# Prologue of a spectral layer with an MLP behind it: first-stage results kept in the memory of later weights, loop data loaded in four pieces, half of batch 2's first stage put into the main loop

## The chip, the core and the metric

One core of one Trainium2 chip runs the whole program. The metric is the device time of one execution in microseconds (us), the median of several runs. The engines are named as in the profile: PE (matmul) and PEld (its weight loads), DVE, ACT, POOL, and SP, which here only issues DMA transfers.

## What is computed

The input x is 4 batches of 3008 positions with 256 channels. Cut to what matters, the reference is:

```python
X = np.fft.rfft(x, axis=1)
Yr = Xr @ w_r - Xi @ w_i + b_r
Yi = Xr @ w_i + Xi @ w_r + b_i
Yr, Yi = softshrink(Yr, 0.01), softshrink(Yi, 0.01)
y = np.fft.irfft(Yr + 1j * Yi, n=3008, axis=1).reshape(12032, 256)
h = y @ w_in                       # 256 -> 2048
P = a[0] + a[1]*h + a[2]*h**2 + a[3]*h**3
Q = 1 + |b[0]|*|h| + |b[1]|*h**2
out = (P / (Q + 1e-6)) @ w_out     # 2048 -> 256
```

The MLP's weights w_in, w_out come as 64-bit floats and are turned on the chip into pairs of 32-bit values (a rounded high part and the rest).

## The kernel before

**The transform.** 3008 = 64 x 47. A batch passes five steps. The first stage (`f1_task`) is a transform over 47 points, 16 tasks of one matmul each, two tasks for each of 8 pieces of x; its result `a` is stored to a DRAM scratch `s1`, since the next step wants other rows on the partitions. `f2_task` (12 tasks) loads `s1` back as `bt`, does the 64-point transform with the table `f2`, and ACT makes a high part, PE (L222) and ACT a low part, and ACT (L218) a negated copy. `m_task` is the complex product with the weights, 24 matmuls and one for the bias, and the soft threshold (ACT L246, DVE L249). `i1_task` transforms back with the table `g1`, and its result `zt` is copied out of PSUM by ACT (L149) and stored to a second scratch `s2`. `i2_task` loads `s2` as `ct` and makes columns of y for the MLP.

**Prologue and main loop.** Batch 1 (`b == 0` in the code) passes f1 to i1 in a prologue, in which the MLP's weights are also loaded and converted (`more_raw` issues loads, `convert(n)` takes n steps of a conversion; 16 conversions of 5 steps; one costs ACT three instructions and DVE four). Its order is written out by hand: for each p from 0 to 14 the code runs f2 of p, m of p-2, i1 of p-3, with `HC[p]` and `HM[p]` conversion steps between. Batch 2 (`b == 1`) has all 16 first-stage tasks in the prologue: two before the loop over p, six in its first three passes, eight behind it. The main loop then runs 208 units (26 blocks of columns x 8 slices of the hidden layer): 12 matmuls L321 into `h`, a rational function on ACT, POOL and DVE, 12 matmuls L412 into `acc`, three units later. The tasks of batches 2 to 4 are dealt out to these units by a budget: each task has a cost in us, and a unit takes tasks until it has its share of the sum, at most two at a time.

**Memory and queues.** Every DMA is issued by SP, in program order, on one queue. The framework gives the queue's transfers eight semaphores in turn, so an issue waits until the eighth transfer before it has landed. Tiles with one tag share a ring of buffers: `zt` has the tag "a" with three buffers in the pool `sm`, so the fourth result waits until the first has been stored. `a` of the prologue has five buffers of its own in the pool `pro` plus two lent places. The weights' tiles (tags "win0" to "win7", "wsp0" to "wsp7") lie in memory for good and are empty until the weights come; pieces 2 to 7 of x use the "win" places already. Before the loop over p, 20 matmuls on zeros (`warm`, L483) keep PE busy.

Of the kernel before, what the change touches and what calls it, by code (L numbers as in the profile page):

```python
# [30 lines left out]
RAWS = (2, 2, 2, 2, 2, 2, 2, 0, 0, 0, 0, 0)  # L31
HC = (0, 3, 3, 4, 4, 4, 4, 4, 4, 4, 4, 4)
HM = (0, 0, 3, 3, 3, 3, 4, 4, 4, 4, 4, 4, 4, 4)
# [62 lines left out]
def spectral_moe(ctx, tc, t, out):  # L96
# [53 lines left out]

    def f1_task(b, i):
# [28 lines left out]
    def load_b(b, p):  # L180
        if b or p < 2:
            bt = sm.tile([128, 2, D], F32, tag="b", name="bt")
        else:
            bt = pro3.tile([128, 2, D], F32, tag="b", name="bt", bufs=4)
# [11 lines left out]
    def f2_task(b, p):  # L196
        ahead = 2 if b else 3
        if p + ahead < NK // 2:
            late.append(lambda: load_b(b, p + ahead))
        bt = b_t.pop((b, p))  # L200
# [17 lines left out]
        nc.scalar.activation(out=every[:, :, :64], in_=v32(every[:, :, 128:]), func=ACTF.Copy, scale=-1.0)  # L218
# [33 lines left out]
    def i1_task(b, p):  # L252
# [8 lines left out]
        copy(0, zt.rearrange("p k d -> p (k d)"), pt.rearrange("p k d -> p (k d)"))  # L261
# [180 lines left out]
    raw_pool = pro_stack.enter_context(tc.tile_pool(name="raw", bufs=max(len(WHOLE), 1)))  # L442
# [30 lines left out]
    with tc.manual_schedule():  # L473
        nc.vector.memset(cb, 1.0)
        nc.scalar.activation(out=cb, in_=cb, func=ACTF.Abs_reciprocal_sqrt)
        nc.sync.dma_start(out=f1, in_=t["f1"])
        idle = pro.tile([128, 512], mybir.dt.bfloat16, tag="idle", name="idle", bufs=1)
# [70 lines left out]
        for i in range(8, 16):  # L548
            drain(f1_task(0, i))
# [8 lines left out]
        nc.sync.dma_start(out=eye, in_=t["minus"])  # L558
        first = fft_tasks(1)
        begin_f1 = [first.pop(0)[3] for _ in range(2)]  # L560
        for g in begin_f1:
            next(g)
            next(g)
        prepare()
        load_b(0, 0)
        load_x(1, 1)
        load_b(0, 1)
        nc.sync.dma_start(out=f2[:, 4:8], in_=f2_src[:, 4:8])
        load_b(0, 2)
        load_x(1, 2)  # L570
        load_x(1, 3)
        for g in begin_f1:
            drain(g)
        more_raw(2)
        warm(20)
        np_ = NK // 2
        for p in range(np_ + 3):
            if p < np_:
# [3 lines left out]
                sl = slice(2 * p + 8, 2 * p + 10)  # L582
                if p < np_ - 4:
                    nc.sync.dma_start(out=f2[:, sl], in_=f2_src[:, sl])
                sl = slice(2 * p, 2 * p + 2)
                nc.sync.dma_start(out=g1[:, sl], in_=g1_src[:, sl])
            if p < 3:
                for _ in range(2):
                    drain(first.pop(0)[3])
# [12 lines left out]
            if p == 3:  # L602
# [147 lines left out]
```

## Time and profile before

| | before |
|---|---|
| median of 3 runs | 1498.27 us (1498.03 to 1498.34) |
| profiled execution | 1502.75 us, its span 1500.9 us |
| PE busy | 1469.2 us, 98% of the span |
| DVE busy | 1377.1 us, 92% |
| ACT busy | 1298.0 us, 86% |
| chain that ended last | PE 83%, DVE 7%, ACT 4%, issue 3%, DMA 2% |

The chain is the work followed back from the last instruction to what released each step. A busy share is a mean over stages with different limits, so a stage's own limit is read from a table of the busy times in that stage.

### The profile page before, as it was taken

The numbers are of one execution on the slowest core, as the hardware profiler recorded it, in microseconds if no ns is written. First come the engines' busy times: TensorE is split into PE (matmuls) and PEld (weight loads), VectorE is DVE, ScalarE is ACT, GpSimd is POOL, SyncE is SP. The second block draws the span as 40 slices with busy tenths as digits, with TensorE's granted clock in tenths as the row PEclk, the third lists the DMA queues.
The fourth block names the chain that finished last, engine by engine and source line by source line (L and its number), as shares of the span: only waits on it lengthen the run. The fifth ranks groups of instructions, "written<-read, shape, count | busy, mean of one in ns | idle before, by whom it ended". The sixth has DMA issues, their size and how long they took to land.

```text
span 1500.9 us, 19717 instructions
## 1 busy us (share of the span) xinstructions
PE 1469.2 (98%) x7335; PEld 1225.8 (82%) x7335; DVE 1377.1 (92%) x1328; ACT 1298.0 (86%) x1550; POOL 470.0 (31%) x218
## 2 busy tenths in 40 slices
PE   8989999999999999999999999999998999999998
PEld 3786999998878999999888998999886777776776
DVE  1563999999999999999999999999999999999998
ACT  4777989888989888898899988998887999999886
POOL 0001233323333233233233323332345333333332
PEclk9999999999999999999999999999999999999999
DMA  8954010111232011011132101011010000000000
GB/s 253 359 157 131 23 55 28 55 43 40 62 114 74 28 42 55 28 56 41 57 111 76 35 28 55 28 35 41 28 40 13 27 14 27 27 13 27 9 13 21
DMA packets 56431, 88.72 MB, mean 59 GB/s; under 512 B 5544, under 2 KB 40176, under 8 KB 56336
## 3 DMA queue, kind: packets, MB, share of 16 engines
q1 hardware_dynamic: 56336, 87.46, 18.8%
q8 instruction: 58, 0.95, 0.3%
q14 instruction: 37, 0.30, 0.1%
HBM read 49.96 MB, written 37.49 MB: 58 GB/s over the span
## 4 chain that ended last, share of the span: by engine, by line
PE 83%; DVE 7%; ACT 4%; issue 3%; DMA 2%; SPq 0%; ACTq 0%; DVEq 0%
PE acc L412 32%; PE h L321 31%; PE pft L240 7%; PE pi L291 3%; PE pft L156 3%; PE pft L204 2%; PE pft L258 2%; DMA s<-a 1%; DVE t L359 1%; DMA xin<-in_x 1%; DVE v L382 1%; DVE t L376 1%; DVE y L384 1%; DVE p L374 1%; PE pm L240 1%
## 5 line engine op out<-in xcount | busy, mean ns | idle before, releaser
L348 POOL TENSOR_TENSOR v<-w,m 128x940 f32<-128x940 f32 (+1 forms) x208 | 456.9, 2196 | 1019.2 <-DVE p L374 485.2
L321 PE MATMUL h<-xsh,win 128*128 128x470 f32 (+1 forms) x1664 | 448.8, 391 | 2.6 <-DVE t L361 2.4
L412 PE MATMUL acc<-g,wsp 128*128 128x470 f32 (+1 forms) x1908 | 433.7, 375 | 5.1 <-DVE g L379 5.1
L412 PEld LDWEIGHTS acc<-g,wsp 128*128 128x128 f32 x1908 | 358.3, 189 | 54.8 <-DVE g L379 7.1
L321 PEld LDWEIGHTS h<-xsh,win 128*128 128x128 f32 x1664 | 303.9, 189 | 61.0 <-issue 20.6
L361 DVE SCALAR_TENSOR_TENSOR t<-t,small,h 128x940 f32<-128x940 f32 (+1 forms) x208 | 244.9, 1177 | 6.1
L346 ACT ACTIVATE w<-m,small 128x940 f32<-128x940 f32 (+1 forms) x208 | 241.6, 1162 | 7.0
L359 DVE TENSOR_TENSOR t<-t,h 128x940 f32<-128x940 f32 (+1 forms) x208 | 231.2, 1111 | 16.4 <-ACT t L347 16.1
L321 PE MATMUL h<-xsl,win 128*128 128x470 f32 (+1 forms) x832 | 242.1, 372 | 0.0
L353 ACT ACTIVATE y<-v 128x940 f32<-128x940 f32 (+1 forms) x208 | 202.8, 975 | 37.0 <-DVE g L379 28.3
L347 ACT ACTIVATE t<-h,small 128x940 f32<-128x940 f32 (+1 forms) x208 | 229.8, 1105 | 0.0
L354 ACT ACTIVATE y<-y 128x940 f32<-128x940 f32 (+1 forms) x208 | 203.8, 980 | 6.6
L344 ACT ACTIVATE m<-h 128x940 f32<-128x940 f32 (+1 forms) x208 | 194.5, 935 | 16.4 <-PE h L321 13.6
L379 DVE TENSOR_TENSOR g<-t,y 128x940 fp32r<-128x940 f32 x159 | 179.5, 1129 | 18.0 <-PE acc L412 16.3
L371 DVE SCALAR_TENSOR_TENSOR g<-t,small,y 128x940 fp32r<-128x940 f32 x159 | 191.9, 1207 | 1.1 <-ACT y L354 1.1
L376 DVE SCALAR_TENSOR_TENSOR t<-t,small,p 128x940 f32<-128x940 f32 x159 | 189.5, 1192 | 0.0
L374 DVE SCALAR_TENSOR_TENSOR p<-v,g 128x940 f32<-128x940 f32 x159 | 179.0, 1126 | 0.1
L321 PEld LDWEIGHTS h<-xsl,win 128*128 128x128 f32 x832 | 155.3, 188 | 20.9 <-DVE xsl L302 0.2
L412 PE MATMUL acc<-g,f 128*128 128x470 f32 (+1 forms) x392 | 155.7, 539 | 2.5 <-DVE g L388 2.5
L412 PEld LDWEIGHTS acc<-g,f 128*128 128x128 f32 x392 | 73.3, 189 | 60.8 <-issue 54.6
L240 PE MATMUL pft<-wrh,x 128*128 128x256 f32 x288 | 75.3, 283 | 0.0
L240 PE MATMUL pft<-wih,x 128*128 128x256 f32 x288 | 75.2, 283 | 0.0
(84 smaller groups left out, 1437.2 us busy)
## 6 DMA issues: line engine op xcount, KB each, us to landing
xin<-in_x SPq DMA_DIRECT2D x32, 384.0 KB, 4.7
s<-a SPq DMA_DIRECT2D x64, 192.0 KB, 3.4
bt<-s SPq DMA_DIRECT2D x48, 256.0 KB, 3.0
s<-zt SPq DMA_DIRECT2D x48, 256.0 KB, 2.2
out_t<-ob SPq DMA_DIRECT2D x50, 235.0 KB, 2.3
ct<-s SPq DMA_DIRECT2D x22, 480.0 KB, 4.2
raw_win<-in_w_in SPq DMA_DIRECT2D x8, 512.0 KB, 6.9
raw_wsp<-in_w_out SPq DMA_DIRECT2D x8, 512.0 KB, 7.1
```

What stands on the lines that cost most here:

```text
L240: nc.tensor.matmul(out=pt[:, k, :], lhsT=l, rhs=r, start=False, stop=n == len(ops) - 1, skip_group_check=True)
L321: nc.tensor.matmul(out=h[:, i, :w], lhsT=l, rhs=r, start=k == 0, stop=k == len(ops) - 1)
L344: nc.scalar.activation(out=d["m"], in_=h, func=ACTF.Abs)
L346: nc.scalar.activation(out=d["w"], in_=d["m"], func=ACTF.Identity, scale=cb[:, 1:2], bias=cb[:, 0:1])
L347: nc.scalar.activation(out=d["t"], in_=h, func=ACTF.Identity, scale=a[:, 3:4], bias=a[:, 2:3])
L348: nc.gpsimd.tensor_tensor(out=d["v"], in0=d["w"], in1=d["m"], op=ALU.mult)
L353: nc.scalar.activation(out=d["y"], in_=d["v"], func=ACTF.Square, bias=C0)
L354: nc.scalar.activation(out=d["y"], in_=d["y"], func=ACTF.Abs_reciprocal_sqrt)
L359: nc.vector.tensor_tensor(out=tt, in0=tt, in1=h, op=ALU.mult)
L361: nc.vector.scalar_tensor_tensor(out=tt, in0=tt, scalar=d["a"][:, 1:2], in1=h, op0=ALU.add, op1=ALU.mult)
L376: stt(out=tt, in0=tt, scalar=a0, in1=p, op0=ALU.add, op1=ALU.subtract)
L412: nc.tensor.matmul(out=acc[n][e][:, :w], lhsT=l[:, e * 128:(e + 1) * 128], rhs=r, start=begun[n] == 1 and k == 0, stop=begun[n] == UB and ...
```

## The change

Eight pieces of `a` of batch 1 (two tasks each, 4 KB a partition) go to the places "wsp0" to "wsp7" and are stored whole, by turns copied by ACT and DVE. No load of batch 2's x stands among them. `bt` of batch 1 is loaded as four tiles `b_all` of six rows each, f2 and g1 in two or three pieces each, and all 16 raw weights, and then pieces 0 to 3 of batch 2's x, are issued ahead of the loop over p. In batch 1 the negated copy goes from ACT to POOL, the copy of `zt` from ACT to DVE. `warm` grows from 20 to 36. Of batch 2's first stage, eight tasks run behind the loop over p, with `a` in the three buffers of "a" in `sm`, and eight are left to the main loop.

```diff
-RAWS = (2, 2, 2, 2, 2, 2, 2, 0, 0, 0, 0, 0)
-HC = (0, 3, 3, 4, 4, 4, 4, 4, 4, 4, 4, 4)
-HM = (0, 0, 3, 3, 3, 3, 4, 4, 4, 4, 4, 4, 4, 4)
+HC = (0, 0, 3, 3, 3, 3, 3, 3, 3, 3, 3, 3)
+HM = (0, 0, 4, 4, 4, 4, 4, 4, 4, 4, 4, 4, 4, 4)
...
-        if b == 0 and i % 7 >= 5:
-            at = const.tile([128, 4, D], F32, tag="win1" if i % 7 == 5 else f"wsp{SPLIT[0]}", name="a")[:96, :2]
+        if b == 0:
+            if not r:
+                a_t[0] = const.tile([128, 4, D], F32, tag=f"wsp{c}", name="a")[:96]
+            at = a_t[0][:, 2 * r:2 * r + 2]
         else:
-            at = (pro if early else sm).tile([128, 2, D], F32, tag="a", name="a", bufs=5 if early else 3)[:96]
-        copy(0, at.rearrange("p j d -> p (j d)"), pt[:96])
+            at = sm.tile([128, 2, D], F32, tag="a", name="a", bufs=3)[:96]
+        copy(i % 2 if b == 0 else 0, at.rearrange("p j d -> p (j d)"), pt[:96])
         yield
         if r:
             del xin[b, c]
-            if c < 6 and b > 1:
-                load_x(b, c + 2)
+            ahead = 4 if b == 1 and c < 4 else 2
+            if b and c + ahead < NJ // 4 and not (b == 1 and c in (2, 3)):
+                load_x(b, c + ahead)
...
-        nc.scalar.activation(out=every[:, :, :64], in_=v32(every[:, :, 128:]), func=ACTF.Copy, scale=-1.0)
+        if b:
+            nc.scalar.activation(out=every[:, :, :64], in_=v32(every[:, :, 128:]), func=ACTF.Copy, scale=-1.0)
+        else:
+            nc.gpsimd.tensor_scalar(out=every[:, :, :64], in0=v32(every[:, :, 128:]), scalar1=-1.0, scalar2=0.0, op0=ALU.mult, op1=ALU.add)
...
-        copy(0, zt.rearrange("p k d -> p (k d)"), pt.rearrange("p k d -> p (k d)"))
+        copy(b == 0, zt.rearrange("p k d -> p (k d)"), pt.rearrange("p k d -> p (k d)"))
...
+        b_all = [pro3.tile([128, 6, D], F32, tag=f"b{z}", name="b_all", bufs=1) for z in range(4)]
...
+        for i in range(16):
+            drain(f1_task(0, i))
+        prepare()
...
+        nc.sync.dma_start(out=f2[:, 4:12], in_=f2_src[:, 4:12])
+        load_all(0)
+        load_all(6)
+        more_raw(2)
+        load_g1(slice(0, 8))
+        nc.sync.dma_start(out=f2[:, 12:], in_=f2_src[:, 12:])
+        load_all(12)
+        more_raw(2)
+        load_g1(slice(8, NK))
+        load_all(18)
...
+        more_raw(len(jobs))
+        for c in range(4):
+            load_x(1, c)
+        warm(36)
...
-        while first[0][0]:
+        for _ in range(8):
             drain(first.pop(0)[3])
-        del first[:2]
-        load_b(1, 0)
-        load_b(1, 1)
```

**The queue of SP around the first results.** In the kernel before, inside the loop over p, a store of `zt` (to `s_472`, which is `s2` of batch 1) stands between the loads of one pass:

```order
L264 DMA s_472<-zt 128x2x256
L185 DMA bt<-s_125 128x2x256
L517 DMA raw_wsp_493<-in_w_out 128x2x256
L517 DMA raw_wsp_495<-in_w_out 128x2x256
L584 DMA f_70<-in_f 128x256
L586 DMA g_71<-in_g 128x256
```

In the changed kernel, at the end of the loads that stand ahead of the loop (`s_428` is `s2` of batch 1, `s_1005` is `s1` of batch 2):

```order
L525 DMA raw_wsp_253<-in_w_out 128x2x256
L525 DMA raw_wsp_255<-in_w_out 128x2x256
L141 DMA xin<-in_x 96x1024 x4
L271 DMA s_428<-zt 128x2x256 x12
L283 DMA ct<-s_428 96x1280
L178 DMA s_1005<-a 96x512
L141 DMA xin<-in_x 96x1024
L178 DMA s_1005<-a 96x512 x2
```

All twelve stores of `zt` now stand behind all loads of weights and four pieces of x, and the stores of batch 2's `a` behind `ct`, with loads of x between them.

**The engine that copies the fourth `zt`.** Before, on ACT, in pass 6 (its waits in brackets: HW3 is the semaphore of the first store):

```order
L246 ACTIVATE yt<-pm 128x512 [waits PE_49]
L469 ACTIVATE win_669<-e 128x2x256 [waits DVE_49]
L214 ACTIVATE x<-pft 128x4x128 [waits PE_49]
L218 ACTIVATE x<-x 128x8x64 [waits Activation_49]
L149 ACTIVATE zt<-pft 128x512 [waits DMAHW3_49,PE_49]
L208 ACTIVATE x<-pft 128x4x128 [waits PE_49]
```

Now, on DVE, in the same pass (HW7 is the semaphore of the first store):

```order
L256 SCALAR_TENSOR_TENSOR yt<-pm,yt 128x512 [waits Activation_49]
L478 TENSOR_TENSOR win_563<-e,win_563 128x2x256 [waits DVE_49]
L465 SCALAR_TENSOR_TENSOR e<-raw_win_237,e 128x512 [waits DMAHW1_49,DVE_49]
L471 ISA e<-e,r 128x1024 [waits DVE_49]
L146 COPY zt<-pft 128x512 [waits DMAHW7_49,PE_49]
L463 TENSOR_SCALAR e<-e 128x512 [waits Activation_49]
L478 TENSOR_TENSOR win_602<-e,win_602 128x2x256 [waits Activation_49]
L465 SCALAR_TENSOR_TENSOR e<-raw_win_239,e 128x512 [waits DMAHW2_49,DVE_49]
L256 SCALAR_TENSOR_TENSOR yt<-pm,yt 128x512 [waits Activation_49]
```

The copy and its wait for the first store have moved to DVE, ahead of the conversions and of the next soft threshold.

**PE where the main loop begins.** Before, from the last eight first-stage tasks (each row x8 is eight matmuls of 512 columns):

```order
L156 MATMUL pft<-xin,small 96x512 x8
L291 MATMUL pi_1146<-small,ct 128x94 x5
L291 MATMUL pi_1152<-small,ct 128x94 x5
L321 MATMUL h<-xsh,win_370 128x470 x4
L321 MATMUL h<-xsl,win_370 128x470 x2
L321 MATMUL h<-xsh,win_370 128x470 x4
L321 MATMUL h<-xsl,win_370 128x470 x2
L204 MATMUL pft<-f_70,bt 128x128 x8
L321 MATMUL h<-xsh,win_427 128x470 x4
```

Now, from the same place:

```order
L157 MATMUL pft<-xin,small 96x512 x8
L298 MATMUL pi_1061<-small,ct 128x94 x5
L298 MATMUL pi_1067<-small,ct 128x94 x5
L328 MATMUL h<-xsh,win_367 128x470 x4
L328 MATMUL h<-xsl,win_367 128x470 x2
L328 MATMUL h<-xsh,win_367 128x470 x4
L328 MATMUL h<-xsl,win_367 128x470 x2
L157 MATMUL pft<-xin,small 96x512 x2
L328 MATMUL h<-xsh,win_387 128x470 x4
```

Eight first-stage tasks stand in both ahead of the loop; the changed kernel has two more in each of units 0 to 3, where the kernel before has second-stage and product tasks of batch 2, which now begin in unit 5.

## Rows read from the trace of the kernel before

**Rows 1.** Busy time of each engine in stretches (start:end, length, then PE, PEld, DVE, ACT and POOL busy us with their instruction counts, granted clock, DMA share, GB/s): the start of the loop over p, its steady part, its end to the first matmul of the main loop, the main loop's first units, the main loop up to the end of batch 4's transform.

```profile
32.70:46.60 13.90, 11.21 (x39) 6.35 (x37) 4.08 (x8) 5.59 (x10) 0.00 (x0) 0.75 1.03 348
46.60:103.70 57.10, 51.16 (x370) 47.74 (x369) 37.34 (x66) 49.34 (x94) 0.00 (x0) 1.00 0.84 273
103.70:125.30 21.60, 20.26 (x100) 14.68 (x99) 5.81 (x10) 11.25 (x21) 0.00 (x0) 0.92 0.42 131
125.30:161.70 36.40, 34.29 (x209) 30.65 (x208) 22.72 (x24) 31.06 (x41) 8.88 (x4) 1.00 0.24 76
161.70:1093.00 931.30, 931.30 (x4909) 825.05 (x4909) 908.25 (x845) 831.77 (x970) 302.54 (x136) 1.00 0.16 50
```

**Rows 2.** Timeline of PE from the last product of batch 1 to the first units: start us, duration us, engine, line, instruction, count, and idle time of the engine before it with what ended it.

```profile
109.19 0.58 PE L233 MATMUL pm<-bias,selr 128*128 128x512 f32 x1
...
115.02 7.03 PE L156 MATMUL pft<-xin,small 96*96 96x512 f32 x16
122.47 1.32 PE L291 MATMUL pi<-small,ct 96*128 96x94 f32 x10 [0.41 <-DMA ct<-s]
...
125.31 0.67 PE L321 MATMUL h<-xsh,win 128*128 128x470 f32 x2
...
130.08 1.13 PE L204 MATMUL pft<-f,bt 128*128 128x128 f32 x8 [1.46 <-DMA bt<-s]
```

**Rows 3.** Timeline of PE over one pass of the loop over p without a wait (columns as in Rows 2).

```profile
61.57 0.47 PE L233 MATMUL pm<-bias,selr 128*128 128x512 f32 x1
...
65.85 1.05 PE L204 MATMUL pft<-f,bt 128*128 128x128 f32 x8
66.66 0.47 PE L233 MATMUL pm<-bias,selr 128*128 128x512 f32 x1
```

**Rows 4.** Timeline of SP, PE and ACT in the first 30 us (columns as in Rows 2).

```profile
1.19 3.87 SPq L142 DMA_DIRECT2D xin<-in_x  x8
...
5.67 9.65 PE L156 MATMUL pft<-xin,small 96*96 96x512 f32 x22 [1.28 <-DMA xin<-in_x]
...
18.65 2.05 ACT L149 ACTIVATE a<-pft 96x512 f32<-96x512 f32 x4 [6.13 <-DMA s<-a]
...
19.30 9.30 PE L156 MATMUL pft<-xin,small 96*96 96x512 f32 x14 [3.97 <-ACT a L149]
```

**Rows 5.** The same table as in Rows 1 for three short stretches: the loads of x, the loads of weights, `bt`, f2 and g1 in the loop, and PE after a wait.

```profile
4.00:16.00 12.00, 10.04 (x23) 3.50 (x22) 0.00 (x0) 4.14 (x7) 0.00 (x0) 1.00 1.04 258
45.00:60.00 15.00, 14.99 (x103) 13.09 (x102) 9.77 (x17) 12.56 (x24) 0.00 (x0) 0.97 1.06 384
40.00:45.00 5.00, 5.00 (x13) 2.89 (x12) 0.71 (x2) 2.30 (x4) 0.00 (x0) 0.50 1.06 390
```

**Rows 6.** DMA issues of three moments, each a window that holds one issue (KB, us from issue to landing): a store of `zt` at 65.64 us with the queue full, one at 102.18 us with the queue empty, a load of `bt` at 29.80 us.

```profile
s<-zt SPq DMA_DIRECT2D x1, 256.0 KB, 6.2
...
s<-zt SPq DMA_DIRECT2D x1, 256.0 KB, 2.1
...
bt<-s SPq DMA_DIRECT2D x1, 256.0 KB, 2.8
```

**Rows 7.** Groups of POOL instructions of the whole program: line, instruction, count, busy us, mean ns of one, idle us before them.

```profile
L717 POOL TENSOR_TENSOR f<-wsp 128x512 f32<-128x512 f32 x6 | 13.2, 2208 | 0.0
```

**Rows 8.** Timeline of ACT at the end of the prologue (columns as in Rows 2).

```profile
115.27 0.60 ACT L149 ACTIVATE zt<-pft 128x512 f32<-128x512 f32 x1 [1.13 <-PE pft L258]
...
123.04 1.56 ACT L149 ACTIVATE a<-pft 96x512 f32<-96x512 f32 x3 [2.93 <-DMA s<-a]
124.49 0.57 ACT L294 ACTIVATE xsh<-pi 128x470 fp32r<-128x470 f32 x1
```

**Rows 9.** Groups of DVE instructions between 46 and 116 us (columns as in Rows 7).

```profile
L464 DVE CUSTOM_DVE_ANT_0 e<-e,r 128x1024 uint16<-128x1024 uint16 x16 | 11.0, 688 | 0.3
L249 DVE SCALAR_TENSOR_TENSOR yt<-pm,yt 128x512 f32<-128x512 f32 x12 | 8.3, 689 | 15.2 <-ACT yt L246 15.2
L456 DVE TENSOR_SCALAR e<-e 128x512 uint32<-128x512 uint32 x15 | 6.3, 421 | 3.5 <-ACT e L453 3.5
L471 DVE TENSOR_TENSOR win<-e,win 128x512 fp32r<-128x512 f32 x8 | 5.5, 690 | 2.7 <-ACT win L469 2.7
...
L458 DVE SCALAR_TENSOR_TENSOR e<-raw_wsp,e 128x512 uint32<-128x512 uint32 x8 | 5.5, 684 | 0.0
```

**Rows 10.** Timeline of SP's queue at the same place.

```profile
118.10 0.33 SPq L276 DMA_DIRECT2D ct<-s  x1
118.47 6.46 SPq L170 DMA_DIRECT2D s<-a  x8
```

**Rows 11.** Timeline of PE from the twelve matmuls of unit 1 to what follows them.

```profile
131.86 1.11 PE L321 MATMUL h<-xsh,win 128*128 128x470 f32 x4
...
134.53 0.63 PE L222 MATMUL pft<-x,minus 128*128 128x512 f32 x2
135.61 0.50 PE L233 MATMUL pft<-bias,selr 128*128 128x512 f32 x1 [0.45 <-ACT x L214]
```

**Rows 12.** Timeline of DVE: the first instruction of a unit's DVE work in units 0, 4 and 5.

```profile
131.92 1.13 DVE L359 TENSOR_TENSOR t<-t,h 128x940 f32<-128x940 f32 x1 [5.12 <-ACT t L347]
...
161.69 1.13 DVE L359 TENSOR_TENSOR t<-t,h 128x940 f32<-128x940 f32 x1
...
168.28 1.13 DVE L359 TENSOR_TENSOR t<-t,h 128x940 f32<-128x940 f32 x1
```

More of the change, by code (lines that the diff above doesn't have):

```diff
@@ L135, in load_x @@
     def load_x(b, c):
-        if b == 1 and c in (2, 3, 6, 7):
-            xt = pro3.tile([96, 4, D], F32, tag=f"x{c % 4}", name="xin", bufs=1)
+        if b == 1 and c in (2, 3):
+            xt = pro3.tile([96, 4, D], F32, tag=f"x{c}", name="xin", bufs=1)
         elif b == 0 and c >= 2:
@@ L149, in copy @@
             nc.scalar.activation(out=out, in_=in_, func=ACTF.Copy)
+    a_t = {}
     def f1_task(b, i):
@@ L166, in f1_task @@
             del xin[b, c]
-            if c < 6 and b > 1:
-                load_x(b, c + 2)
+            ahead = 4 if b == 1 and c < 4 else 2
+            if b and c + ahead < NJ // 4 and not (b == 1 and c in (2, 3)):
+                load_x(b, c + ahead)
+        if b == 0:
+            if r:
+                nc.sync.dma_start(out=s1[b].rearrange("k g c j d -> (k g c) j d")[:, 4 * c:4 * c + 4, :], in_=a_t[0])
+            return
         o = 4 * c + 2 * r
@@ L180, in load_b @@
     def load_b(b, p):
[L181 to L184, printed above, removed]
+        bt = sm.tile([128, 2, D], F32, tag="b", name="bt")
         nc.sync.dma_start(out=bt, in_=s1[b][2 * p:2 * p + 2].rearrange("k g c j d -> (g c j) k d"))
@@ L196, in f2_task @@
     def f2_task(b, p):
[L197 to L200, printed above, removed]
+        if b and p + 2 < NK // 2:
+            late.append(lambda: load_b(b, p + 2))
+        bt = b_t.pop((b, p)) if b else b_all[p // 3][:, 2 * (p % 3):2 * (p % 3) + 2]
         pt = bank(b, "f2" if p % 2 else "").rearrange("p (z f) -> p z f", z=4)
@@ L441, in spectral_moe @@
     pro3 = pro_stack.enter_context(tc.tile_pool(name="pro3", bufs=3))
-    raw_pool = pro_stack.enter_context(tc.tile_pool(name="raw", bufs=max(len(WHOLE), 1)))
+    raw_pool = pro_stack.enter_context(tc.tile_pool(name="raw", bufs=len(WHOLE))) if WHOLE else None
     pro2 = pro_stack.enter_context(tc.tile_pool(name="pro2", bufs=2))
@@ L539, in spectral_moe @@
         nc.sync.dma_start(out=f2[:, :4], in_=f2_src[:, :4])
-        load_x(1, 0)
-        for i in range(8):
-            drain(f1_task(0, i))
         wts = []
@@ L547, in spectral_moe @@
             wts.append(wt)
-        for i in range(8, 16):
-            drain(f1_task(0, i))
         sel = pro.tile([4, 130], F32, tag="sel", name="sel", bufs=1)
@@ L558, in spectral_moe, with load_all, load_g1 @@
         nc.sync.dma_start(out=eye, in_=t["minus"])
-        first = fft_tasks(1)
[L560 to L576, printed above, removed]
+        for i in range(16):
+            drain(f1_task(0, i))
+        prepare()
+        np_ = NK // 2
+        def load_all(k):
+            nc.sync.dma_start(out=b_all[k // 6], in_=s1[0][k:k + 6].rearrange("k g c j d -> (g c j) k d"))
+        def load_g1(sl):
+            nc.sync.dma_start(out=g1[:, sl], in_=g1_src[:, sl])
+        nc.sync.dma_start(out=f2[:, 4:12], in_=f2_src[:, 4:12])
[8 more added lines that the diff above has]
+        load_all(18)
+        nc.sync.dma_start(out=ca, in_=t["a"].rearrange("(o d) -> o d", o=1).to_broadcast([128, 4]))
+        nc.sync.dma_start(out=cb, in_=t["b"].rearrange("(o d) -> o d", o=1).to_broadcast([128, 2]))
+        nc.sync.dma_start(out=i2, in_=t["i2"])
+        more_raw(len(jobs))
+        for c in range(4):
+            load_x(1, c)
+        warm(36)
+        first = fft_tasks(1)
         for p in range(np_ + 3):
@@ L581, in spectral_moe @@
                 next(f2g)
[L582 to L589, printed above, removed]
             flush()
             if p < np_:
-                more_raw(RAWS[p])
                 convert(HC[p])
@@ L601, in spectral_moe @@
                 drain(i1_task(0, p - 3))
-            if p == 3:
-                nc.sync.dma_start(out=ca, in_=t["a"].rearrange("(o d) -> o d", o=1).to_broadcast([128, 4]))
-                nc.sync.dma_start(out=cb, in_=t["b"].rearrange("(o d) -> o d", o=1).to_broadcast([128, 2]))
-                nc.sync.dma_start(out=i2, in_=t["i2"])
-            if 6 <= p < 10:
-                load_x(1, p - 2)
             if p == 8:
@@ L611, in spectral_moe @@
         flush()
-        more_raw(len(jobs))
         while running or len(done) < len(jobs):
```

## The prediction

> **What bounds the kernel now.** First read the table of busy times by stage [rows 1]. From 161.7 to 1093 us PE is busy for all of its time (931.30 of 931.30 us), with DVE close behind (908.25). There, work added to PE counts in full. Ahead of it stand a prologue of 125.3 us, in which no engine is full, and the first units, where PE idles 36.40 - 34.29 = 2.1 us. The prologue is where a new order can gain. Its PE work at full clock is small: two times sixteen first-stage tasks at 7.03 / 8 = 0.88 us [rows 2], twelve passes at 66.66 - 61.57 = 5.1 us [rows 3] and 2.2 us of i2, about 91 us. So some 34 us are lost: a start of 5.7 us, a wait of 4.0 us for a store that holds a buffer [rows 4], waits and half clock from 32.7 to 46.6 us (clock 0.75 [rows 1]), and shorter waits behind.
>
> **First stage and its stores.** The waits of ACT (6.13 us) and PE (3.97 us) for `s<-a` [rows 4] go, as eight places hold all of `a`. What is late next is the queue. The eight pieces of x (3.15 MB) arrive at 258 GB/s [rows 5], from about 4 to 16.2 us, as before. Then follow 0.26 MB of f2, 0.52 MB of weights and 3.15 MB of stores: at the 384 GB/s of the busy stretch [rows 5] 10.2 us, landed at about 27. The first quarter of `b_all` (0.79 MB) needs all stores. A load of 0.26 MB took 2.8 us [rows 6], so 2.1 us besides its bytes; with 2.0 us of bytes it lands at 31. The loop begins where it begins now, near 32; what is gained is that nothing of batch 2 stands in it.
>
> **The queue behind it.** In the order now, the first store of `zt` stands behind every weight and four pieces of x. After 31 us there are 13.1 MB (three quarters of `b_all`, 16 raw weights, g1, the rest of f2): 34.1 us at 384 GB/s, so 65. Four pieces of x at 258 GB/s add 6.1 us, the store's own bytes 0.7 and its landing 1.0: it lands at **73 us**. That the queue works in order rests on two stores of the same size, 6.2 us from issue to landing with others ahead, 2.1 us with none [rows 6]. Bounds: 70 us if x moves at 384 GB/s too and the gap ahead of the first quarter is filled; 81 us if all pieces with rows of 4 KB or more (stores, f2, g1, 6.0 MB) move at the 258 GB/s of x.
>
> The Trainium skill, "DMA: Bandwidth & Descriptors", section Bandwidth, says "Batch DMAs to ≥1 MiB for ≥75% of peak" and lists 425 GB/s for 16 MB. The trace differs: pieces of 128 to 512 KB already ran at 384 GB/s. By that best rate, as an estimate, the store would land near 66 us and the whole would come to 1499 us; rival 4 is this.
>
> **The wait that it makes.** Passes without a wait take 5.1 us [rows 3]. The first product begins near 35 us (second stage 1.0, two copies 1.3, the negated copy on POOL 1 to 2.2 [rows 7]). The fourth `zt` comes at the end of pass 6, near 60 us; the fifth raw weight, 7.3 MB behind the first quarter of `b_all`, lands near 50 us and pass 4 asks for it near 48, which makes it 61 or so. Its copy on DVE must wait for the first store: 73 - 61 = 12 us. Behind it on DVE are queued nine conversions and the soft thresholds of the next passes; PE gets one second stage and one product further (4 us) and then needs the bank that this copy empties, so PE stands for some 8 us.
>
> After 73: copy 0.6, i1 0.9, four passes 20.4, a pass without second stage 4.0, and from the last product to the last copy 115.87 - 109.19 = 6.7 us [rows 2, 8]: 32.6 us. PE comes from a wait: after one of 3.97 us, 14 matmuls took 9.30 us instead of 6.2 [rows 4], and the clock was 0.50 in such a stretch [rows 5]. That adds 3 us, 35.6 in all. DVE's own sum is below it: nine conversions of 0.42 + 3 x 0.69 us, the last step of a tenth, seven thresholds of 0.69 [rows 9], nine copies of 0.6 give 33 us. So the last copy of `zt` ends at 108.6 us, against 115.87 now [rows 8]: **-7.3 us**. The moves from ACT to POOL and DVE cost nothing here: ACT loses work in each pass, and DVE comes to 0.69 + 0.6 + 1.4 conversions of 2.5 us = 4.8, under PE's 5.1; the negated copy is used two passes later; with a full POOL (2.2 us a copy) only the first product feels it, ahead of the 12 us wait that swallows it.
>
> **From there to the main loop.** Now 125.31 - 115.87 = 9.4 us [rows 2, 8]: the store lands 2.2 us after the copy (`ct` is issued at 118.10 [rows 10]), `ct` 4.3 us later, the first `a` 0.6 after it (ACT goes on at 123.04, after 2.93 us for `s<-a` [rows 8]). In the changed kernel three buffers in place of five serve eight tasks, and two pieces of x at 1.5 us stand between the stores. So counted from the last copy: first `a` landed at 7.1, x 8.6, second and third `a` 9.1 and 9.6, x 11.1, fourth 11.6 us. The seventh copy waits for that fourth, the eighth follows, then ACT makes xsh: first L321 at 13.6 us, **+4.2 us** (0 if the stores overtook x, 6 if PE is at half clock throughout).
>
> **In the main loop.** Eight tasks move into it: 7.0 us [rows 2]. PE has no free time after the first units, so **+7.0**; what could hide it is PE's idle time there, and that grows instead. Units 0 to 2 hold 134.53 - 131.86 = 2.7 us [rows 11] of L321 and 1.8 us of first stage, 4.5 us of PE against a step of 168.28 - 161.69 = 6.6 us that DVE sets [rows 12]; now second stages and products fill them, save waits of 1.46 and 0.45 us [rows 2, 11]. Stepping the units on (DVE's first at 131.92 - 125.31 = 6.6 us, then ACT and DVE at 4.5 to 6.6), PE is full again 33 us after the first L321 with 28 us of work done: 5 us idle against 2.1, **+3.0**. The first matmuls may run at half clock: **+1** (0 to 3).
>
> **Sum.** -7.3 + 4.2 + 7.0 + 3.0 + 1.0 = +7.9 us. The profiled execution (1502.75 us, span 1500.9) lies 4.5 us above the median; a difference is the same on both, so on the median 1498.27 it gives **1506 us**.
>
> **Rivals.** (1) The other side, faster: the early loads are free and the first store doesn't hold the fourth copy, since small stores get through among the loads. The point is whether it lands before 61 us. Then the last copy ends at 35 + 3.3 + nine passes 45.9 + 4.0 + 6.7 + 2 of half clock = 97 us, -19 + 15.2 = -3.8: 1494.5 us. For it: the copies in the loop now never wait for a store. Against it: 20 MB stand ahead of the store, and stores with others ahead took 6.2 us [rows 6]. The Trainium skill ("DMA: Bandwidth & Descriptors", Rules for kernel authors: issue the DMA early, wait on its semaphore late) speaks for this case; it says nothing of what queues behind. (2) The moved tasks fall into PE's idle time: 7 us less, 1499 us. Against it is PE at 931.30 of 931.30 us. (3) The queue is slower, with 4 KB rows at 258 GB/s: everything 8 us later, 1514 us. For it: x itself moves so. (4) Merged pieces move faster than split ones. The fastest stretch in the rows had 390 GB/s [rows 5], 0.8 us earlier, so 1505 us; no row gives more, and to come within 3 us of no change the store would have to land at 68 us.
>
> **How the numbers follow.** Forecast 0.56; rival 1 0.14; rival 2 0.14; rival 3 0.12; rival 4, with 68 us or less, 0.04. What a measurement here can tell from no change is about 0.2%, 3 us: 1495.3 to 1501.3. Faster: two thirds of rival 1 (0.09) and the lower end of rival 2 (0.03), 0.12. Same: the rest of rival 1 (0.05), most of rival 2 (0.09) and of rival 4 (0.03), and the forecast's lower end (0.03: landing at 70 us and no half clock take 6 us off), 0.20. Slower: the rest, 0.68. Range: from the lower end of rival 2 (1496.5) to rival 3 (1514), which leaves out most of rival 1 and what lies above rival 3.
>
> **What would show it.** In the changed profile: DVE's copy of `zt` (L146) idle some 12 us until a DMA `s<-zt`, near 61 to 73 us, and PE idle some 8 us just after, then half clock; the last copy near 109 us; ACT's copies of batch 2's `a` waiting for `s<-a` for over 4 us; first L328 near 122 us; PE with about 5 us idle in units 0 to 4. Wrong if the copy doesn't wait or the first L328 comes before 115 us.

## The result and the profile after

| | before | after |
|---|---|---|
| time, median (us) | 1498.30 (1498.03 to 1499.58) | 1515.38 (1514.80 to 1516.34) |
| ratio, 95% interval | | 1.0108 [1.0093, 1.0124] |
| profiled execution, its span (us) | 1502.75, 1500.9 | 1515.74, 1513.9 |
| last `zt` copy ends | 115.87 | 113.51 |
| first main-loop matmul (L321; after: L328) | 125.31 | 127.86 |
| from there to the span's end | 1375.6 | 1386.1 |

The change costs 17.1 us, 1.1%. The forecast was 1506; its range ended at 1514. Lines of after: first stage L157, second stage L208, `zt` copy L146 (DVE), its matmul L265, i2 L298, first layer L328.

The stages of after, in the table of [rows 1, 5]:

```profile
31.00:66.00 35.00, 30.96 (x224) 29.71 (x225) 21.14 (x36) 21.16 (x38) 4.67 (x6) 0.95 1.06 382
66.00:76.00 10.00, 2.03 (x14) 1.51 (x13) 1.34 (x3) 3.19 (x6) 0.62 (x1) 0.73 0.99 276
76.00:82.00 6.00, 5.06 (x23) 4.65 (x24) 5.39 (x10) 2.29 (x5) 0.62 (x1) 0.60 0.16 55
82.00:113.50 31.50, 28.97 (x201) 26.18 (x201) 24.59 (x44) 18.53 (x34) 3.40 (x4) 1.00 0.15 50
113.50:127.90 14.40, 10.83 (x35) 6.45 (x33) 1.95 (x4) 5.65 (x10) 0.00 (x0) 0.79 0.77 233
127.90:180.00 52.10, 49.86 (x236) 39.22 (x235) 41.24 (x38) 46.00 (x56) 16.23 (x8) 0.96 0.26 76
180.00:1100.00 920.00, 920.00 (x4875) 815.50 (x4875) 885.16 (x824) 816.03 (x956) 294.09 (x132) 1.00 0.17 51
```

The second row is the new thing. For ten microseconds PE is busy for 2.03, DVE for 1.34, and the DMA engines for all of the time: everybody waits for a transfer. Behind it PE works for 6 us at a granted clock of 0.60. The waits of the first 130 us say who waits for what (engine, line, what ended the wait: us in total, times, longest us):

```profile
DVE zt L146 <- DMA s<-zt: 8.8, 1, 8.8
...
PE pft L265 <- DVE zt L146: 8.0, 2, 7.3
ACT a L148 <- DMA s<-a: 6.7, 3, 4.8
...
PE pft L208 <- DMA b_all<-s: 4.6, 1, 4.6
...
PE pft L157 <- ACT a L148: 3.6, 1, 3.6
```

The timelines of DVE and PE and the one transfer that was issued at 65.20 us (KB, us to landing) show the same in order of time:

```profile
66.68 0.69 DVE L471 CUSTOM_DVE_ANT_0 e<-e,r 128x1024 uint16<-128x1024 uint16 x1
76.19 0.69 DVE L146 COPY zt<-pft 128x512 f32<-128x512 f32 x1 [8.82 <-DMA s<-zt]
```

```profile
76.94 2.07 PE L265 MATMUL pft<-yt,g 128*128 128x256 f32 x4 [7.31 <-DVE zt L146]
```

```profile
s<-zt SPq DMA_DIRECT2D x1, 256.0 KB, 10.9
```

The first store of `zt` is issued at 65.20 and lands 10.9 us later, at 76.1; with an empty queue such a store takes 2.1 us [rows 6]. Its tile was ready at 51.4 us. SP, which issues in program order, came to the store only behind the last loads of weights and the four of x, and issued it when the eighth transfer before it had landed (65.12). So the store loses 13.8 us ahead of its issue and 10.9 behind it. The fourth `zt` needs its place, DVE stands until then, and PE behind DVE.

The tail, from the last `zt` copy on, in the timelines of PE and ACT, to be held against [rows 2, 8]:

```profile
112.97 5.39 PE L157 MATMUL pft<-xin,small 96*96 96x512 f32 x12 [1.26 <-DVE zt L146]
121.92 2.02 PE L157 MATMUL pft<-xin,small 96*96 96x512 f32 x2 [3.57 <-ACT a L148]
123.74 4.42 PE L298 MATMUL pi<-small,ct 96*128 96x94 f32 x20
127.86 2.10 PE L328 MATMUL h<-xsh,win 128*128 128x470 f32 x4
```

```profile
114.74 1.77 ACT L148 ACTIVATE a<-pft 96x512 f32<-96x512 f32 x3
121.28 0.59 ACT L148 ACTIVATE a<-pft 96x512 f32<-96x512 f32 x1 [4.77 <-DMA s<-a]
```

In before, the second half of i2 was

```profile
124.17 1.35 PE L291 MATMUL pi<-small,ct 96*128 96x94 f32 x10 [0.38 <-ACT a L149]
```

In after, the first copies fill the three places; the copy at 121.28 has waited 4.77 us for a store, PE's last two matmuls behind it 3.57, and i2, which took 1.32 + 1.35 us in before, takes 4.42: after the wait PE runs at the lower clock, 0.50 granted from 121.9 to 127.9 us.

The kernel before isn't the same from one execution to the next. Its 59 executions beside the experiments lie between 1497.9 and 1503.1 us, those up to 1499 us with a mean granted clock of 0.997 to 0.999, the longest with 0.993. The profiled one, at 1502.75 us, belongs to the long end. Their median is 1500.2 us, 1.9 above the median in the table, which rests on four executions; whether the chip or the draw makes that isn't shown. Held against it the change costs 15 us.

### The profile page after: what moved, and what is told of

The parts are those of the page before. It is cut to its first block, busy times and chain, and to the rows that moved or that the text cites. A ratio compares the mean times of both kernels' runs of the same rounds, so it can differ in the third digit from the quotient of the medians.

```text
span 1513.9 us, 19716 instructions
## 1 busy us (share of the span) xinstructions
PE 1475.7 (97%) x7350; PEld 1231.3 (81%) x7351; DVE 1390.6 (92%) x1348; ACT 1281.5 (85%) x1518; POOL 479.3 (32%) x230
## 4 chain that ended last, share of the span: by engine, by line
PE 84%; DVE 5%; issue 3%; ACT 3%; DMA 1%; ACTq 0%; DVEq 0%
PE acc L419 33%; PE h L328 32%; PE pft L247 7%; PE pi L298 4%; PE pft L208 2%; PE pft L265 2%; PE pft L157 2%; DVE t L366 1%; DMA s<-zt 1%; DVE t L383 1%; PE pi L229 1%; DVE p L381 1%; PE pft L229 1%; PE pm L247 1%; PE pft L240 1%
## 5 line engine op out<-in xcount | busy, mean ns | idle before, releaser
L328 PE MATMUL h<-xsh,win 128*128 128x470 f32 (+1 forms) x1664 | 450.6, 392 | 3.2 <-DVE t L368 3.2
L328 PEld LDWEIGHTS h<-xsh,win 128*128 128x128 f32 x1664 | 304.8, 190 | 64.8 <-issue 21.2
L328 PE MATMUL h<-xsl,win 128*128 128x470 f32 (+1 forms) x832 | 242.6, 373 | 0.0
L328 PEld LDWEIGHTS h<-xsl,win 128*128 128x128 f32 x832 | 155.7, 188 | 20.8
```

The costliest lines, as they stand in the source:

```text
L328: nc.tensor.matmul(out=h[:, i, :w], lhsT=l, rhs=r, start=k == 0, stop=k == len(ops) - 1)
```

## The experiments

Ratios are to runs of the kernel before on the same chip (medians 1500.07 to 1500.37 us there), with 95% intervals. The kernel after was not run again there, so where a time is held against after's 1515.38 us, some 2 us are open; the stretches in the traces are the surer reading. "Main loop" is from the first L328 (L321) to the span's end, "tail" from the last `zt` copy to it.

**The kernel before again.** No edit.

> The kernel before, unchanged, profiled once more. Two readings of why the profile of before (1502.75 us) and the profile of after (1515.74 us) lie 13.0 us apart and the medians 17.1 us: (A) the profile of before lay some 4.5 us above what the kernel takes, and the excess lies in one stretch, so that a second profile comes out near 1498.5 us and shows which stretch is shorter; (B) profiling adds 4 to 5 us to this kernel and not to the other, and the second profile reads 1502 to 1503 us again, with the same stage times. The timed runs should read 1498 to 1499 us either way, ratio 1.000.

1499.31 us, 1.0002 [0.9993, 1.0011]; its profiled execution took 1501.63. The last `zt` copy ended at 113.92 us, 1.95 us earlier than in the first profile, and the first product began at 42.8 us instead of 46.6 (later steps lost half of it again); main loop 1376.4. Neither reading holds as put: profiling adds nothing (other executions read as much), and the excess is no fixed stretch. It comes and goes in the prologue, where the clock does: the first profile has 0.50 at 40 to 45 us [rows 5], the second full clock there.

**Seven places for zt.**

```diff
-        zt = sm.tile([128, 2, D], F32, tag="a", name="zt", bufs=3)
+        zt = (pro3.tile([128, 2, D], F32, tag="zt", name="zt", bufs=7) if b == 0 else sm.tile([128, 2, D], F32, tag="a", name="zt", bufs=3))
```

> The kernel after, with the twelve results zt of batch 2's partner (the first batch's last stage) in seven places of their own instead of the three that they share, so that the fourth zt copy needs no store to have landed. Theory T1 (the store of the first zt, queued behind all loads and landed at 76.1 us, holds the fourth copy for 8.8 us and TensorE for 7.3 us): that wait and the half clock behind it go, the loop ends 7 to 10 us earlier, the total is 1505 to 1508 us. Rival R1 (VectorE's and GpSimd's work after the stall has to be done anyway and bounds the loop's end): the last zt copy moves by under 2 us and the total stays at 1513 to 1515 us. Rival R2 (the loads bound it: what is queued ahead of the store is also what the next products need): a wait for another transfer takes the place of the store's, total 1512 to 1515 us.

1506.31 us, 1.0048 [1.0036, 1.0061]: 9 us less than after. The wait for `s<-zt` is gone, and the last copy ends at 105.27. The first store still lands at 76.3, so it is the place that made it matter. Tail 14.2, main loop 1387.3, as in after.

**Seven places for a.**

```diff
-            at = sm.tile([128, 2, D], F32, tag="a", name="a", bufs=3)[:96]
+            at = (pro3.tile([128, 2, D], F32, tag="at", name="a", bufs=7) if early else sm.tile([128, 2, D], F32, tag="a", name="a", bufs=3))[:96]
```

> The kernel after, with the eight results a of batch 2 that are made in the prologue in seven places of their own instead of three shared with zt. The stall of the fourth zt copy stays. Theory T2 (the tail between the last zt copy and the main loop's first matmul takes 14.3 us instead of 9.4 because each a waits for a store to leave one of three places: 6.7 us of ScalarE in three waits): first main-loop matmul at 122.5 to 124 us instead of 127.7, total 1510 to 1512 us. Rival R3 (the tail waits for the load of ct, landed at 120.6 us, and the a's are done beside it): first main-loop matmul stays within 1.5 us of 127.7, total 1514 to 1516 us.

1515.48 us, 1.0103 [1.0087, 1.0118], tail 13.9: by the numbers the rival. But ACT's timeline shows another wait in its place:

```profile
121.85 0.59 ACT L148 ACTIVATE a<-pft 96x512 f32<-96x512 f32 x1 [2.16 <-DMA s<-a]
127.49 1.02 ACT L301 ACTIVATE xsh<-pi 128x470 fp32r<-128x470 f32 x2 [5.04 <-DMA s<-a]
```

The new places lie in a prologue pool, whose memory the main loop's tiles take over; xsh then waits for the stores to leave it. So this run decided nothing, and the next one put the places where they stay.

**Six shared places.**

```diff
-            at = sm.tile([128, 2, D], F32, tag="a", name="a", bufs=3)[:96]
+            at = sm.tile([128, 2, D], F32, tag="a", name="a", bufs=6)[:96]
```

The same for zt and for the output tile ob.

> The kernel after, with six instead of three places for the tiles that a, zt and ob share. With seven places for zt alone the stall went and the total fell to 1506.3 us, and the tail (last zt copy to first main-loop matmul) stayed at 14.2 us; seven places for a alone left it at 13.9 us, but there the wait may only have moved, since those places lay under the main loop's pools, and xsh then waited 5.0 us for the stores. Here the places belong to a pool that lives on. Theory T1+T2 (both costs are waits for shared places): loop's end at 105 to 106 us, tail 9.5 to 11.5 us, total 1502 to 1504 us. Rival R3 (the tail is the load of ct and what follows it): tail 13 to 14.5 us, total 1505.5 to 1507.5 us.

1503.27 us, 1.0018 [1.0009, 1.0026]: 12 us less than after. Last copy at 104.55, tail 11.5, main loop 1384.5. Both waits were for places: some 9 us of the stall, 3 of the tail.

**The x loads later.**

```diff
-        for c in range(4):
-            load_x(1, c)
...
+            if 5 <= p < 9:
+                load_x(1, p - 5)
```

> The kernel after, with the four loads of batch 2's input (393 KB each) issued one by one from the sixth to the ninth step of the loop instead of ahead of it. Three places for zt as in after. Theory T1 (the fourth zt copy waits for a store that stands in line behind every load issued before it): with four loads fewer ahead of it the first store lands 4 to 6 us earlier (70 to 72 us instead of 76.1) and the copy with it; total 1508.5 to 1511.5 us, some two thirds of the way to the kernel with seven places. Rival R2 (the store itself takes that long, or the line doesn't hold it in order): the landing stays at 75 to 77 us, total 1514 to 1516 us.

1509.81 us, 1.0064 [1.0051, 1.0077], 5.6 us less than after. DVE's timeline and the store issued at 60.37 us:

```profile
70.50 0.69 DVE L146 COPY zt<-pft 128x512 f32<-128x512 f32 x1 [0.89 <-DMA s<-zt]
```

```profile
s<-zt SPq DMA_DIRECT2D x1, 256.0 KB, 10.0
```

It lands at 70.4. With four loads fewer ahead the landing and the fourth copy come 5.7 us earlier, the last copy 5.9 and the whole 5.6: the store stands in line behind the loads, and what it is late the kernel is late.

**Half the first stage left to the main loop of before.**

```diff
...
-            if 6 <= p < 10:
+            if 6 <= p < 8:
                 load_x(1, p - 2)
...
-        while first[0][0]:
-            drain(first.pop(0)[3])
-        del first[:2]
-        load_b(1, 0)
-        load_b(1, 1)
```

The last two pieces of x are then loaded by the main loop's tasks.

> The kernel before, with the second half of batch 2's first stage (eight tasks of one matmul, one copy and one store each) left to the main loop, and nothing else changed but the places of two x loads. Theory T3 (the tasks cost the TensorE-bound main loop their own time, 7.0 us, and 3 us of idle in its first units, and free at most 1.5 us of a tail that waits for the load of ct anyway): total 1505 to 1509 us. Rival R4 (the main loop takes them in its gaps): total 1496 to 1499 us. If the main loop of after was longer for another reason than the eight tasks, the main loop here (first matmul to last) is as long as in before within 2 us.

1509.81 us, 1.0072 [1.0060, 1.0085]. Main loop 1386.3, as long as in after, with the prologue of before.

**All sixteen in the prologue of after.**

```diff
+        elif b == 1 and c >= 4:
+            xt = pro3.tile([128, 6, D], F32, tag=f"b{c - 4}", name="xin", bufs=1)[:96, :4]
...
+            if p in (5, 8, 11, 14):
+                load_x(1, 4 + (p - 5) // 3)
...
-        for _ in range(8):
+        for _ in range(16):
             drain(first.pop(0)[3])
+        del first[:2]
+        load_b(1, 0)
+        load_b(1, 1)
```

> The kernel after, with all sixteen tasks of batch 2's first stage done at the loop's end, none in the main loop; the four x loads that this takes go into the places of the loop data that has been used. Three shared places as in after. Theory T3 (the eight tasks cost the main loop 10.3 us, their own 7.0 and more around them): first to last main-loop matmul 1375 to 1377 us as in before instead of 1386, the tail longer by 7.0 us of TensorE and up to 3 us of waits for places, total 1512 to 1515 us. Rival R4 (the main loop's 10 us come from what stands around it, the x loads or the state that the prologue leaves): main loop 1383 us or more, total 1519 us or more.

1514.04 us, 1.0092 [1.0078, 1.0105]. Main loop 1374.9; tail 22.9, 8.6 more than in after. With the run above: the eight tasks cost the main loop 10 to 11 us, whichever prologue precedes it.

**Stores of a in smaller pieces.**

```diff
-        if b == 0:
-            if r:
-                nc.sync.dma_start(out=s1[b].rearrange("k g c j d -> (k g c) j d")[:, 4 * c:4 * c + 4, :], in_=a_t[0])
-            return
```

What follows, the store of two columns that the other batches use, then serves the first batch too.

> The kernel after, with the first batch's a stored in sixteen pieces of 2 KB a row instead of eight of 4 KB a row. Theory T4 (the rows of 4 KB made the stores slow: 1.36 us each, 289 GB/s, where shorter rows moved at 384 GB/s): the sixteen pieces take 0.5 to 0.6 us each, the first b_all lands 1.5 to 2.5 us earlier than 33.4 us, and everything behind it, the stall's end too: total 1513 to 1514 us. Rival R5 (writing at that pitch is as slow in either shape, or the sixteen issues cost what the rows give): first b_all at 33 to 34 us, total 1515 to 1517 us.

1516.49 us, 1.0106 [1.0091, 1.0122]; `b_all` issued at 28.38 us, as in after (28.49), and landed at 35.1, later than either theory had it. Rows of half the length moved no faster: 286 to 337 GB/s in the windows from 17 to 25 us, 309 to 338 in after. And in the kernel before, stores with the same rows of 2 KB moved at 398 GB/s from 18 to 21 us. So longer rows aren't what makes the stores slow.

**The copies back on ACT.** And the negation of x for the first batch, again ACT's as for the others.

```diff
-        copy(b == 0, zt.rearrange("p k d -> p (k d)"), pt.rearrange("p k d -> p (k d)"))
+        copy(0, zt.rearrange("p k d -> p (k d)"), pt.rearrange("p k d -> p (k d)"))
```

> The kernel after with the first batch's zt copy and the negation of x back on ScalarE, as in before. Theory (both moves are hidden: nothing on the path waited for either engine but at the stall, which is the store's): total 1514.5 to 1516.5 us, the stall at the same place, now a wait of ScalarE. Rival R9 (ScalarE, 27 to 29 us busy of the loop's 75 outside the stall, gets late for the products' x copies or for the conversions): loop's end 1 to 3 us later, total 1516.5 to 1518.5 us.

1517.79 us, 1.0115 [1.0101, 1.0129]; last copy at 115.95. By the numbers that is the rival, but the intervals of this and after overlap, and in this trace the first product already came 1.7 us later (39.3 against 37.6); whether the moves brought 2 us or nothing isn't settled. The stall stays, as a wait of ACT.

**Both remedies together.** The edits of six shared places and of all sixteen tasks (the last x piece loaded in step 12 of the loop).

> The kernel after with six shared places and with all sixteen tasks of batch 2's first stage done at the loop's end: the two remedies together. Main loop 1375 us instead of 1384.5; loop's end at 104.5 to 105.5 us as with six places alone; the tail longer by the eight tasks: with three places they made it 8.5 us longer, with six I expect 7 to 8 us, so 18.5 to 19.5 us. Theory (the costs add up and are independent): 1500 to 1502 us, level with before. Rival R6 (with six places the tail's stores still hold the last tasks): tail 21 us or more, total 1503 us or more.

1497.48 us, 0.9981 [0.9972, 0.9990]. Last copy 104.90, tail 15.4 (I had 18.5), main loop 1375.6. The tails with eight tasks (six shared places alone) and here with sixteen, in the table of [rows 1]:

```profile
104.50:116.10 11.60, 9.95 (x35) 6.18 (x33) 1.99 (x4) 5.30 (x10) 0.00 (x0) 0.82 0.83 265
```

```profile
104.90:120.30 15.40, 14.78 (x50) 6.76 (x49) 1.48 (x3) 9.72 (x18) 0.00 (x0) 1.00 0.85 264
```

With eight tasks PE waits 1.65 us for `ct` ahead of i2, and i2 takes 4.44 us at a granted clock of 0.50. Sixteen tasks keep PE busy until i2, which takes 2.37 us at full clock. So the tail is 3.9 us longer than with eight tasks, not 7.

**Eight of them within the loop.** As the last kernel, with eight tasks left at the loop's end.

```diff
+            if 7 <= p < 11:
+                for _ in range(2):
+                    drain(first.pop(0)[3])
```

> As the kernel with six places and all sixteen tasks, but the first eight tasks stand two by two in steps 8 to 11 of the loop instead of at its end, so that their stores are gone before the tail. Theory (TensorE's own time is what they cost, 7.0 us, wherever they stand, and only the tail's waits differ): loop's end at 111.5 to 113 us, tail 11.5 to 12.5 us, main loop 1375 us, total 1499.5 to 1501.5 us. Rival R7 (VectorE and ScalarE in these steps have no room for eight copies, or the banks of PSUM wait): loop's end past 114 us, total 1502 us or more.

1508.02 us, 1.0046 [1.0034, 1.0059]. Last copy at 119.72, 15 us later than with six places alone, for 7 us of matmuls: the rival, and worse. Among the waits PE stands 3.2 and 3.0 us for DVE to empty a bank, ACT 2.3 for `s<-zt`; a and zt again share the six places before the first store has landed, and from 75 to 107 us the clock is 0.89. How much each of these costs wasn't taken apart.

**Six places in the kernel before.**

```diff
-        zt = sm.tile([128, 2, D], F32, tag="a", name="zt", bufs=3)
+        zt = sm.tile([128, 2, D], F32, tag="a", name="zt", bufs=6)
```

The same for the main loop's a and for ob.

> The kernel before with six instead of three shared places for zt, for the main loop's a and for the output tile (its prologue's a keep five places of their own). With six places the main loop of after was 1384.5 us long instead of 1386.1. Theory (the gain sits in the first units, where the eight leftover tasks wait for places, and before has no such tasks): main loop 1375.5 to 1376.5 us, total within 0.5 us of before. Rival R8 (the output tiles or the other batches' a wait for places too): main loop 1374 to 1375 us, total 1 to 2 us below before.

1500.50 us, 1.0000 [0.9991, 1.0009]; main loop 1376.3. More places are worth nothing where nothing waits for them.

**The last copies on ACT.**

```diff
-        copy(b == 0, zt.rearrange("p k d -> p (k d)"), pt.rearrange("p k d -> p (k d)"))
+        copy(b == 0 and p < 9, zt.rearrange("p k d -> p (k d)"), pt.rearrange("p k d -> p (k d)"))
```

> The kernel after, with the last three of the twelve zt copies (products 10 to 12) on ScalarE, the first nine on VectorE as in after. From the last product to the last copy after takes 8.6 us, before 6.7 [rows 2, 8]; in after the last two copies stand on VectorE behind five conversion instructions. Theory T5 (1.9 us of the loop's end is that line on VectorE, which the forecast left out): last product to last copy 6.5 to 7.2 us, total 1513 to 1514.5 us. Rival R10 (TensorE's own order sets it, the copies only follow): 8.3 us or more, total 1515 to 1516 us.

1513.72 us, 1.0086 [1.0071, 1.0100]. The interval overlaps that of after, so the reading rests on the trace: from the last product (105.8) to the last copy's end 7.1 us, in after (from 104.9) 8.6. DVE in after, and ACT here:

```profile
109.58 0.68 DVE L471 CUSTOM_DVE_ANT_0 e<-e,r 128x1024 uint16<-128x1024 uint16 x1
110.18 0.42 DVE L463 TENSOR_SCALAR e<-e 128x512 uint32<-128x512 uint32 x1
111.02 0.69 DVE L478 TENSOR_TENSOR wsp<-e,wsp 128x512 fp32r<-128x512 f32 x1 [0.42 <-ACT wsp L476]
111.63 0.68 DVE L465 SCALAR_TENSOR_TENSOR e<-raw_wsp,e 128x512 uint32<-128x512 uint32 x1
112.23 1.28 DVE L146 COPY zt<-pft 128x512 f32<-128x512 f32 x2
```

```profile
111.29 0.63 ACT L476 ACTIVATE wsp<-e 128x512 fp32r<-128x512 f32 x1 [1.42 <-DVE e L471]
111.83 1.07 ACT L148 ACTIVATE zt<-pft 128x512 f32<-128x512 f32 x2
```

In after, the last two copies stand in line behind four conversion instructions on the engine that they were moved to.

**The mixing weights behind the stores.** Together with these weights (`wt`), the small loads `sel` and `bsb` and the unit matrix `eye` move behind the tasks.

```diff
+        for i in range(16):
+            drain(f1_task(0, i))
         wts = []
         for nm in ("w_r", "w_i"):
...
-        for i in range(16):
-            drain(f1_task(0, i))
         prepare()
```

> The kernel after, with the loads of the two mixing weights (0.52 MB), the small ones and the unit matrix issued behind the eight stores of a instead of ahead of them. In after the first store begins only when they are in (18.2 us). Theory T6 (the stores are held by what stands ahead in line, and move at their 1.36 us each from then on): stores landed at 26 to 27 us instead of 28.4, first b_all at 31 to 32 instead of 33.4, the store that ends the stall 0 to 0.5 us earlier, since the same bytes stand ahead of it; total 1514.5 to 1515.5 us. Rival R11 (the stores wait for the making of a): landed at 28 us or later, first b_all no earlier; total 1515 to 1517 us.

1513.41 us (1510.19 to 1515.93), 1.0088 [1.0072, 1.0103], again not clear of after. The stores landed at 26.5 us instead of 28.4, `b_all` at 32.6 instead of 33.4, the store that ends the stall at 75.4 instead of 76.1. Counted from the last x, whose arrival varies between executions (15.3 us in after, 17.0 here, 14.9 to 16.5 in the other traces with this prologue), `b_all` lands 15.6 us later instead of 18.1, and the store that ends the stall 58.4 instead of 60.8.

**All remedies.** Six places, sixteen tasks, the last three copies on ACT and the mixing weights behind the stores.

> The kernel with six shared places and all sixteen tasks in the prologue (1497.5 us), with both of the changes above as well: last three zt copies on ScalarE, the mixing weights loaded behind the stores. Here no stall takes the early gain back: if T5 and T6 hold, loop's end at 101 to 103 us instead of 104.9, total 1494 to 1496 us. If only one holds, 1495.5 to 1497 us; if neither, 1497 to 1498 us.

1493.20 us, 0.9956 [0.9942, 0.9970]: 0.44% faster than before, 22 us faster than after. `b_all` lands at 30.2, the last copy ends at 100.07, main loop 1375.7. The last two edits bring 4.3 us here; what each of them brings wasn't taken apart. Its tail, and the stores of a in some windows, here and then in after (table of [rows 1]):

```profile
17.00:19.00 2.00, 2.00 (x6) 0.75 (x5) 0.69 (x1) 0.88 (x2) 0.00 (x0) 1.00 1.04 422
19.00:21.00 2.00, 2.00 (x11) 0.78 (x8) 0.69 (x1) 0.20 (x1) 0.00 (x0) 1.00 1.01 412
...
100.10:115.70 15.60, 15.07 (x50) 6.73 (x49) 1.91 (x4) 9.70 (x18) 0.00 (x0) 1.00 0.82 261
```

```profile
17.00:19.00 2.00, 2.00 (x6) 0.81 (x5) 0.69 (x1) 0.88 (x2) 0.00 (x0) 1.00 1.04 338
19.00:21.00 2.00, 2.00 (x6) 0.65 (x5) 0.69 (x1) 0.88 (x3) 0.00 (x0) 1.00 0.98 332
23.00:25.00 2.00, 1.95 (x10) 0.88 (x9) 1.84 (x8) 0.00 (x0) 0.00 (x0) 1.00 1.00 311
```

PE is busy for 15.07 of the tail's 15.60 us, at full clock.

## Why the prediction failed where it did

The direction and the mechanism held: the queue in order, the fourth copy that waits for the first store, the tail, the tasks that the main loop has no room for. Two steps failed, and together they make all but a few tenths of the 9.4 us between 1506.0 and 1515.4. In the profiles the terms are

| term | forecast | from profile to profile |
|---|---|---|
| last `zt` copy | -7.3 | 113.51 - 115.87 = -2.4 |
| tail | +4.2 | 14.35 - 9.44 = +4.9 |
| main loop | +7.0 + 3.0 + 1.0 = +11.0 | 1386.1 - 1375.6 = +10.5 |
| sum | +7.9 | +13.0 |

**The first failed step: "So the last copy of `zt` ends at 108.6 us".** It ended 4.9 us later, in two parts. The first is the landing of the store, at 76.1 instead of 73. The stores of a were worked at 384 GB/s ("landed at about 27"). That rate was one of loads; the stores moved at 338 to 309 GB/s in the windows from 17 to 25 us and landed at 28.4, 1.4 us late. The first `b_all` then took 4.9 us from issue to landing instead of the 4.1 worked out for it, and landed at 33.4 instead of 31; 0.7 us came behind that. Loading the mixing weights behind the stores got 2.5 us back, counted from the last x in one trace each.

The other 1.8 us came after the landing, 37.4 us instead of 35.6. "The moves from ACT to POOL and DVE cost nothing here" took DVE's sum, which is below PE's, but not its order at the end, where the last copies stand behind conversions and PE has nothing else: 1.5 us, which three copies on ACT brought back.

The waits themselves were right in kind and smaller than forecast: 8.8 us of DVE for 12, 7.3 of PE for 8, as the fourth copy was ready at 67, not at 61. That the copy was this late is a miss too, which the wait covered: 2.6 us of it stood already in the first product (37.6 for 35), the rest wasn't taken apart. With seven places, where no copy waits for a store, the fourth starts at 68.1 and the last ends at 105.3, not at the 97 of rival 1. So the held copy costs 113.5 - 105.3 = 8.2 us of the loop's end; by the forecast's end and rival 1's it would have been 108.6 - 97 = 11.6.

**The second failed step: "a difference is the same on both".** The sum was made against a profiled execution 4.5 us above the median and then carried to the median. That holds for stretches that both kernels share. The excess lay in the prologue, which the change rewrites: its last copy came at 115.87 us in one profile, 113.92 in the next, 111.54 in the kernel with more places. Against such a shorter execution the change gains nothing up to the last copy: 113.51 is 2 us later than 111.54. The profile of after lies 0.4 us above its own median, so this step is 4.1 of the 9.4 us (with the 4.9 of the first, 0.7 of the tail and -0.5 of the main loop 9.2). The median was part of it: it came from three executions, and the 59 beside the experiments have theirs at 1500.2, 2.5 us below the profile. The range, too, was laid around the median and took in no spread of the stretch to be replaced.

**The main loop** was right in sum. Shown are 10.5 us from profile to profile, and that they go with the tasks and not with the prologue. Their split was not as put: PE's idle time in the first units is 52.10 - 49.86 = 2.2 us, hardly above the 2.1 of before, in place of 3.0 more, and the granted clock of 0.96 there, half clock for about 0.08 x 52.1 = 4.2 us, costs up to 2.1, in place of 1.0. With the 7.0 us of work that makes some 9.2; the last microsecond stays open.

**The tail** was right in size, and in cause for the larger part: six places took 3 of its 4.9 us away. The 2 us that are left are nearly all i2 at the lower clock, 4.44 us there for the 2.67 of before, which the forecast had only in its bound of 6. The order of x among the stores was left as it was in that run, so its part isn't shown.

**The rivals.** Rival 1 fell with the landing at 76.1 us; that late store did hold the copy. Rival 2 fell with the two runs that moved the tasks alone. Rival 3, a slower queue by 4 KB rows, came nearest in time (1514), but that is luck: its store was to land at 81 us, and rows of half the length were no faster. Rival 4 fell: the stretch with the large pieces moved at 382 GB/s (31 to 66 us), the busy stretch of before at 384 [rows 5].

## What to carry to other kernels

A load that is issued early is free only if nothing small that a place depends on stands behind it in the same queue: work out when the first store lands, and give its tiles as many places as there are steps until then. Places must lie in memory that nobody else takes over next, or the wait moves to the new owner. And where a change rewrites a stretch that varies between executions, work its time out against several of them, since a difference taken from one long execution isn't the one that the median will show.

## What the runs showed of the hardware

Eight stores of 393 KB moved at 309 to 338 GB/s (17 to 25 us of after) when half a megabyte of mixing weights, three small loads and the unit matrix stood ahead of them. With these behind, the windows from 17 to 21 us had 422 and 412 GB/s with all remedies, and 409 and 422 in the run with this edit alone. There the next two windows had 322 and 229 with stores still moving; SP issued one store every 1.72 us, as the pieces of a were made, which is 229 GB/s and may be what bounds them there. Rows of 2 KB in place of 4 were no faster. Whether it is the small loads, or that the stores are issued into a full queue, stays open.

The granted clock fell to the lower of its two levels (1.2 GHz) behind the longer waits of PE: it was 0.60 from 76 to 82 us after the 7.3 us stall, and 0.50 in i2 after 3.57 us of waiting in the tail (1.65 us with six places), where i2 took 4.42 us for 2.67. With sixteen first-stage tasks in a tail with six places, PE busy for 14.78 of 15.40 us and the clock at 1.00, eight more tasks cost 3.9 us in place of 7.
